# One score bank per slot instead of any free bank, and at most one VectorE job per round, in an attention planner

## The chip, the cores and the metric

The kernel runs on one core of one Trainium2 chip. The metric is the device time of one execution in microseconds (us). Before the change the median of three runs is 837.48 us (837.4 to 837.57). TensorE is called PE here, VectorE DVE, ScalarE ACT, GpSimd POOL, and SyncE, which issues nearly all DMAs, SP.

## What is computed

The input is x of 2048 rows (tokens) by 640 columns in bf16. It is layer-normalised, goes through an attention layer of 32 heads of 20 columns, through a gated feed-forward part, and the two results are joined:

```
xn  = layernorm(x)
q, k, v = split(xn @ wqkv)                  # 32 heads, 20 columns each
p   = softmax(q @ k.T * 20 ** -0.5)         # per head, 2048 x 2048
s   = (p @ v) @ wo
g   = silu((sigmoid(xn @ w_gate) * (xn @ w_up)) @ w_down)    # inner width 1728
out = x + s * g
```

The costly part is the exponential: 32 heads x 2048 x 2048 = 134 million of them.

## The kernel before

**The unit of work.** Heads are handled in eight groups of four (GH = 4), queries in four chunks of 512 (QC). One group with one chunk is a block, and there are 32 blocks (NBLK). In a block each head has 16 key tiles of 128 keys, so a block has 64 jobs and the kernel 2048. A job is one score matmul of 32 contraction rows by 512 columns (`score_mm`, L836 to L838), which fills one PSUM bank of 128 x 512 floats. The four heads of a group sit on four different groups of 32 rows, so up to four score matmuls of different heads run side by side on PE; this bundle is called a **round** (or F, as in the code). Then one of two engines takes the exponential of the bank:

- ACT, with an ACTIVATE that reads PSUM and writes `pt` in bf16 (`exp_act`, L87, recorded at L83);
- DVE, with one TENSOR_SCALAR that turns the score into 16-bit integers `iv` (L1168), and, for every four of those, three more passes over 2048 columns (L922, L925, L928) which make a product of two bf16 tiles `pb` from the bits.

The weighted sum of values is accumulated on PE in one bank `oacc` for the whole block (PV, `pv_emit`, L864 to L878), again four heads side by side, one matmul per ACT job and two per DVE job.

**PSUM.** There are eight banks: two pairs `scA[0]` and `scA[1]`, which hold two jobs each for ACT (a *slot*; the rounds alternate between them, `nfill % 2`), three single banks `bank[0..2]` (the trace calls them `bk`), and `oacc`. A round puts two jobs into its slot's pair, and ACT handles the pair with one ACTIVATE of 1024 columns. If a single bank is to be had, the round gives ACT a third job there, which costs a second ACTIVATE of 512 columns (L1144 to L1146). DVE's jobs use the same three single banks, and so does every other matmul of the kernel (called M): the projections of q, k and v, the gate, up and down projections of the feed-forward part, and the output projection.

**The planner.** The order of PE, ACT and DVE is not written out by hand. From L1026 on, a loop runs at build time through a clock of its own in steps of 0.02 us; it knows a planned cost for every operation (L422 to L428), keeps in `flex[f]` the planned time at which single bank f becomes free, and emits an instruction on an engine when that engine is free by its clock. On the chip each engine then runs its own list in order and waits on semaphores for what it needs. So a plan only sets order and places; the chip's durations set the time. On PE the choice is made at L1239 to L1252: a round F is issued at once when the margin until ACT runs dry is under URGENT = 0.25 us; otherwise PE stays in its mode (M or PV) while there is work, or holds for a moment when a slot is about to come free.

**What a round takes (L1253 to L1290).** First DVE jobs: up to D_MAX = 2 per round, while DVE is expected to be free in time, each in the first free bank of the list (2, 1, 0) (D_BANKS), picked by `claim_dve` (L827), for a head that the round does not have yet. Then a third bank for ACT, if fewer than two DVE jobs were taken: the first free one of (own, other, 2), where own is bank 0 or 1 by the slot's parity (A_BANKS). Then `claim_act` (L812) takes two or three jobs. So a round has at most four score matmuls: two and a third and a DVE job, or two and two DVE jobs. M items pick their bank at L1224 from (2, 1, 0) (M_BANKS). When the round could wait up to WAIT3 = 0.4 us for one of the banks in A_BANKS, L1243 lets it.

**The end.** After the last PV (chain at L981) the last block is divided on chip: copy of `oacc` (L962), four transposes (L966), scaling (L716, L718), transposes back (L975), copy (L979), then the output projection of the last chunk (L953, L957) and the final products.

Of the kernel before, what the change touches and what calls it, by code (L numbers as in the profile page):

```python
# [30 lines left out]
URGENT, ROUNDS, HOLD, SLACK, LEAD, LAG, D_LAST, D_LAST_END = 0.25, 4, 0.15, 0.2, 40.0, 0.0, 20, 8  # L31
D_ORD, M_ORD, WAIT3, FALL, M_END = 1, 0, 0.4, 1, 0.3
NPT, NPB, NIV = (3, 7), 3, 3
D_MAX, SLACKS = 2, (0.2, 0.2)
A_BANKS, D_BANKS = ((0, 1, 2), (1, 0, 2)), ((2, 1, 0), (2, 1, 0))
M_BANKS = ((2, 1, 0), (2, 1, 0))

LOG2E = 1.4426950408889634
UNIT = 128.0
# [13 lines left out]
def kernel(  # L53
# [33 lines left out]
    def exp_act(o, i):  # L87
        return act_imm(o, i, ACT.Exp, exp_scale)
# [338 lines left out]
    def t_exp(n):  # L427
        return (0.052 if n < SLOT else 0.104) + 0.4267 * n  # L428
# [378 lines left out]
    def take(b, j, i):  # L807
        n_left[b] -= 1
        claimed[0] += 1
        return b, left[b][j].pop(i), j  # L810

    def claim_act(n, not_j):  # L812
        got = []
        for b in range(base(), NBLK):
            if q_at.get(b, 1e9) > now:
                break
            while len(got) < n:
                js = [j for j in range(GH) if left[b][j] and j not in not_j and all(x[2] != j for x in got)]
# [8 lines left out]
    def claim_dve(had, not_j):  # L827
        for b in range(base(), min(NBLK, base() + 2)):
            if q_at.get(b, 1e9) > now:
                return None  # L830
            if n_left[b] >= (D_LAST if b < NBLK - 1 else D_LAST_END):
                js = [j for j in range(GH) if left[b][j] and j not in not_j]
                return take(b, max(js, key=lambda j: (j not in had, len(left[b][j]), j)), -1) if js else None
        return None

    def score_mm(dst, b, kt, j):  # L836
# [180 lines left out]
    with tc.manual_schedule(engines={ENG.PE, ENG.Activation, ENG.DVE}):  # L1017
# [60 lines left out]
        while chain or items or glu_items or any(it.i < len(it.ops) for it in active):  # L1078
# [34 lines left out]
            for eng in ("ACT", "DVE"):  # L1113
# [20 lines left out]
                if eng == "ACT":  # L1134
                    s = slots[nexp % 2]
                    if nexp < nfill and s["a"] is not None and s["at"] <= now:
                        jobs = s["a"]
                        m = len(jobs)
                        w = 2 if m <= 2 and buf_free(pt_left[2], NPT[0]) else 3
                        if buf_free(pt_left[w], NPT[w - 2]):  # L1140
                            pt = w2.tile([P, w, QC], BF16, tag=f"pt{w}", bufs=NPT[w - 2], name=f"pt{w}")
                            if m == SLOT:
                                flex[s["third"]] = now + t_exp(1) + EL
                            if m == SLOT:  # L1144
                                exp_act(pt[:, 2, :], bank[s["third"]])
# [61 lines left out]
            if free["PE"] <= now:  # L1207
# [10 lines left out]
                if cur is None:  # L1218
                    own = nfill % 2
                    m_new, m_bank = None, None  # L1220
                    m_it = next((e for e in active if e.i < len(e.ops) and e.ops[e.i][0] == "PE" and e.ready <= now), None)
                    if m_it is None:
                        behind = done < due() + LAG
                        for f in ((2,) if not behind and claimed[0] < NJOB * NBLK and not (FALL and not pv_ok and not can_f) else M_BANKS[own]):  # L1224
                            if flex[f] <= now:
                                m_bank = f
                                break
                        if m_bank is not None:
                            m_it = next((x for x in items[:80] if x.at <= progress() and (
                                x.need is None or o_at.get(x.need, 1e9) <= now) and all(  # L1230
                                ev_at.get(e, 1e9) <= now for e in x.pre)), None)
# [21 lines left out]
                if nxt == "F":  # L1253
                    busy = max(0.0, free["DVE"] - now) + T_IV * len(dq)
                    own = nfill % 2
                    d_new = []
                    while len(d_new) < D_MAX and (dcur is not None or buf_free(iv_left, NIV)) \
                            and busy + T_IV * len(d_new) <= T_F + T_MODE + PL + SLACKS[len(d_new)]:
                        f = next((f for f in D_BANKS[own] if flex[f] <= now), None)
                        if f is None:  # L1260
                            break
                        x = claim_dve([t[2] for t in dcur["jobs"]] if dcur else [], [y[2][2] for y in d_new])
                        if x is None:
                            break
                        if dcur is None:
                            iv_left.append([1, 0.0])
                            dcur = dict(jobs=[], n=0, k=0, i=len(iv_left) - 1,
                                        iv=w2.tile([P, GH, QC], I16, tag="iv", bufs=NIV, name="iv"))
# [7 lines left out]
                    if jobs or d_new:  # L1276
                        for x, t in enumerate(jobs):
                            score_mm(scA[nfill % 2][:, x, :] if x < 2 else bank[third], *t)
                        end = now + T_F + (T_MODE if mode != "F" else 0.0)
                        for d, i, x, f in d_new:  # L1280
                            score_mm(bank[f], *x)
                            dq.append((d, i, f, end + PL))
                        if jobs:
                            s["a"], s["at"], s["ends"] = jobs, end + PL, 0.0
                            if len(jobs) == SLOT:
                                s["third"] = third
                                flex[third] = 1e9
# [79 lines left out]
```

## Time and profile before

| what | value |
|---|---|
| median of three runs | 837.48 us |
| profiled execution, its own time | 837.4 us |
| its span, first to last instruction | 835.7 us |
| mean granted TensorE clock | 0.993 |
| ACT busy, 100 to 700 us | 99.2 to 100% in each 100 us |
| DVE busy, 100 to 700 us | 90 to 95% |
| PE busy, 100 to 700 us | 95 to 98% |
| first exponential starts, last one ends | 33.0 us, 816.06 us |
| last DMA-free work on POOL ends | 832.8 us |

The table is read so: the kernel has a prologue of 33 us (layer norm, first projections), a long middle in which ACT, DVE and PE all work at once, and an epilogue of 20 us after the last exponential. "Busy" in this profile is the time between an instruction's start and its end, and instructions of one engine overlap, so a busy share close to 100% does not by itself say that an engine is the bound.

### The profile page before, as it was taken

To read this page: it belongs to the slowest core of one execution; us is meant where nothing else is said; L and a number is where in the kernel's file an instruction comes from. 1 tells how busy PE (TensorE), PEld (TensorE's weight loads), DVE (VectorE), ACT (ScalarE), POOL (GpSimd) and SP (SyncE) were. 2 spreads that over 40 slices of the span, in tenths; PEclk is the share of its full clock that TensorE was granted. 3 is DMA by queue.
4 is the path that set the end of the run, shared out by engine and by line. 5 is a ranking of instruction groups with operands and counts; after the bars stand their busy time and mean duration, and the time that the engine had idled before them with its cause. 6 is when DMAs were issued, how large, how long until landed. Compare 5 with 4: busy or idle time off the path is not lost.

```text
span 835.7 us, 16970 instructions
## 1 busy us (share of the span) xinstructions
PE 783.8 (94%) x6388; PEld 277.6 (33%) x6388; DVE 756.3 (91%) x1174; ACT 800.7 (96%) x1043; POOL 81.3 (10%) x90
## 2 busy tenths in 40 slices
PE   4799999999999999999999999999999999999985
PEld 3433223333333232333323222334333333233332
DVE  7678989999899989899899998999999899999993
ACT  7799999999999999999999999999999999999990
POOL 5000000000000000000000000000000002222041
PEclk9899999999999999999999999999999999999998
DMA  5712221122222232221113222322112222324331
GB/s 155 212 35 58 64 67 54 52 67 55 66 75 58 66 85 77 55 66 56 42 43 87 73 62 69 91 78 82 47 62 69 79 72 75 94 61 127 94 130 36
DMA packets 93587, 62.58 MB, mean 75 GB/s; under 512 B 35044, under 2 KB 86884, under 8 KB 93504
## 3 DMA queue, kind: packets, MB, share of 16 engines
q1 hardware_dynamic: 93216, 61.16, 25.9%
q8 instruction: 50, 0.82, 0.4%
q10 hardware_dynamic: 288, 0.33, 0.1%
q14 instruction: 33, 0.27, 0.1%
HBM read 46.51 MB, written 12.40 MB: 70 GB/s over the span
## 4 chain that ended last, share of the span: by engine, by line
ACT 52%; PE 26%; DVE 13%; issue 7%; DMA 1%; SPq 1%; POOLq 0%; POOL 0%; ACTq 0%; DVEq 0%
ACT pt L83 47%; PE scA L837 7%; PE oacc L874 5%; DVE iv L1168 4%; PE bk L654 4%; PE bk L692 3%; ACT tnh L83 3%; DVE pb L928 2%; DVE pb L922 2%; DVE pb L925 2%; PE bk L517 1%; PE bk L742 1%; ACT td L83 1%; PE psk L143 1%; PE bk L625 1%
## 5 line engine op out<-in xcount | busy, mean ns | idle before, releaser
L83 ACT ACTIVATE pt<-scA 128x1024 bf16<-128x1024 f32 x689 | 710.5, 1179 | 6.4 <-PE bk L837 3.5
L1168 DVE TENSOR_SCALAR iv<-bk 128x512 int16<-128x512 f32 x464 | 312.1, 681 | 38.8 <-PE bk L837 37.1
L837 PE MATMUL scA<-q,kT 32*128 32x512 bf16 x1375 | 268.6, 383 | 15.9 <-ACT pt L83 10.6
L837 PE MATMUL bk<-q,kT 32*128 32x512 bf16 x673 | 211.8, 383 | 2.0 <-DVE iv L1168 1.0
L874 PE MATMUL oacc<-pt,v 128*21 128x512 bf16 x1584 | 185.8, 383 | 0.6 <-ACT pt L83 0.4
L837 PEld LDWEIGHTS <-kT 32*128 32x128 bf16 x2048 | 85.3, 91 | 254.8 <-issue 240.3
L83 ACT ACTIVATE pt<-bk 128x512 bf16<-128x512 f32 x209 | 157.5, 754 | 1.3 <-PE bk L837 1.2
L874 PE MATMUL oacc<-pb,v 128*21 128x512 bf16 x928 | 148.4, 382 | 3.4 <-DVE pb L928 2.0
L928 DVE TENSOR_TENSOR pb<-iv,pb 128x2048 bf16<-128x2048 bf16 x116 | 149.5, 1289 | 0.6
L654 PE MATMUL bk<-xnT,wgu 128*128 128x512 bf16 x520 | 145.8, 382 | 1.6 <-DVE hT L662 0.4
L904 POOL TENSOR_TENSOR on_bf<-on,rl 128x512 bf16<-128x512 f32 x31 | 41.0, 1321 | 676.2 <-DMA rl<-rd 498.0
L692 PE MATMUL bk<-wd,hT 128*128 128x320 bf16 x448 | 85.9, 302 | 1.5 <-DVE iv L1168 0.9
L922 DVE TENSOR_SCALAR pb<-iv 128x2048 int16<-128x2048 int16 x116 | 84.0, 724 | 2.1
L874 PEld LDWEIGHTS <-v 128*21 128x21 bf16 x2512 | 51.0, 91 | 95.7 <-issue 73.1
L925 DVE TENSOR_SCALAR pb<-iv 128x2048 int16<-128x2048 int16 x116 | 82.5, 711 | 0.0
L654 PEld LDWEIGHTS <-wgu 128*128 128x128 bf16 x520 | 38.3, 97 | 66.6 <-issue 45.5
L692 PEld LDWEIGHTS <-hT 128*128 128x128 bf16 x448 | 34.5, 97 | 45.8 <-issue 37.7
L517 PE MATMUL bk<-xnT,wu 128*120 128x512 bf16 x160 | 48.7, 398 | 0.2 <-ACT pt L83 0.2
L83 ACT ACTIVATE tnh<-bk 128x512 bf16<-128x512 f32 (+1 forms) x56 | 42.7, 762 | 0.1
L662 DVE SCALAR_TENSOR_TENSOR hT<-tnh,bk 128x512 bf16<-128x512 bf16 x52 | 35.4, 680 | 5.7 <-PE bk L654 3.1
L625 PE MATMUL bk<-wv,xnT 128*128 128x160 bf16 x280 | 30.2, 243 | 1.5 <-DVE iv L1168 1.2
L752 POOL TENSOR_TENSOR xnT<-otmp,xnT 128x320 bf16<-128x320 f32 x24 | 23.3, 975 | 50.8 <-DVE otmp L749 45.3
(105 smaller groups left out, 375.4 us busy)
## 6 DMA issues: line engine op xcount, KB each, us to landing
rl<-rd SPq DMA_DIRECT2D x124, 64.0 KB
wgu<-in_B_w_gate_dram SPq DMA_DIRECT2D x24, 320.0 KB
wgu<-in_B_w_up_dram SPq DMA_DIRECT2D x24, 320.0 KB
gq_dram<-gqs SPq DMA_DIRECT2D x32, 160.0 KB
xnT<-gq_dram SPq DMA_DIRECT2D x12, 320.0 KB
xt<-in_A_x_dram SPq DMA_DIRECT2D x16, 160.0 KB
oU<-on_bf SPq DMA_DIRECT2D x108, 20.0 KB
wd<-in_B_w_down_dram SPq DMA_DIRECT2D x1, 2080.0 KB
```

What stands on the lines that cost most here:

```text
L83: return nc.scalar.add_instruction(mybir.InstActivation(func=func, name=nc.get_next_instruction_name(), engine=ENG.Activation, ins=[nc.sca ...
L517: nc.tensor.matmul(st["ps"][0:UC, :], lhsT=wus[u][:, kd, i, :], rhs=xnT[:, c, kd, :], start=(kd == 0), stop=(kd == KD - 1))
L625: nc.tensor.matmul(st["ps"][:, i * 2 * GC:(i + 1) * 2 * GC], lhsT=xn_tok(tts[i], kd), rhs=wvs[pr][:, kd, :], start=(kd == 0), stop=(kd == ...
L654: nc.tensor.matmul(st[key][0:fs, :], lhsT=w[:, i, kd, ko * P:ko * P + fs], rhs=xnT[:, c, kd, :], start=(kd == 0), stop=(kd == KD - 1))
L692: nc.tensor.matmul(st["ps"][:, 0:HD], lhsT=hT[0:fsz[kf], kf, t4 * P:(t4 + 1) * P], rhs=wd[0:fsz[kf], kf, h * HD:(h + 1) * HD], start=(kf = ...
L837: nc.tensor.matmul(dst, lhsT=kTs[gc(b)[0] % 2][32 * j:32 * j + 32, kt * P:(kt + 1) * P], rhs=qts[b % 3][32 * j:32 * j + 32, :], start=True ...
L874: nc.tensor.matmul(oacc[32 * j:32 * j + DH + 1, :], lhsT=lhsT, rhs=u["src"], start=first, stop=last, tile_position=(0, 32 * j), skip_group ...
L904: nc.gpsimd.tensor_tensor(out=on_bf, in0=on, in1=rl, op=ALU.mult)
L922: nc.vector.tensor_scalar(out=pb[:, 0, :, :].bitcast(I16), in0=iv, scalar1=0x7F80, scalar2=1, op0=ALU.bitwise_and, op1=ALU.bitwise_or)
L925: nc.vector.tensor_scalar(out=pb[:, 1, :, :].bitcast(I16), in0=iv, scalar1=0x007F, scalar2=0x3F00, op0=ALU.bitwise_and, op1=ALU.bitwise_or)
L928: nc.vector.tensor_tensor(out=pb[:, 1, :, :], in0=iv.bitcast(BF16), in1=pb[:, 1, :, :], op=ALU.mult)
L1168: nc.vector.tensor_scalar(out=d["iv"][:, j, :], in0=bank[bk], scalar1=B_OFF, scalar2=0.0, op0=ALU.add, op1=ALU.max)
```

## The change

The change replaces the lists of allowed banks by one fixed choice, and the loop over DVE jobs by a single one:

- A third ACT job may only use the bank of its own slot's parity (bank 0 or 1), and only if the DVE job of the same round did not take it. Bank 2 and the other parity's bank are no longer offered.
- A round takes at most one DVE job, in the first free bank of (2, own, other), where it took up to two from (2, 1, 0).
- An M item looks through (2, other, own) where it looked through (2, 1, 0).
- The short wait before a round looks at its own bank alone.

```
-D_MAX, SLACKS = 2, (0.2, 0.2)
-A_BANKS, D_BANKS = ((0, 1, 2), (1, 0, 2)), ((2, 1, 0), (2, 1, 0))
-M_BANKS = ((2, 1, 0), (2, 1, 0))
...
                             if m == SLOT:
-                                flex[s["third"]] = now + t_exp(1) + EL
+                                flex[nexp % 2] = now + t_exp(1) + EL
                             if m == SLOT:
-                                exp_act(pt[:, 2, :], bank[s["third"]])
+                                exp_act(pt[:, 2, :], bank[nexp % 2])
...
-                        for f in ((2,) if not behind and claimed[0] < NJOB * NBLK and not (FALL and not pv_ok and not can_f) else M_BANKS[own]):
+                        for f in ((2,) if not behind and claimed[0] < NJOB * NBLK and not (FALL and not pv_ok and not can_f) else [(2, 1 - own, own), (2, own, 1 - own)][M_ORD]):
...
-                elif can_f and (margin < URGENT or (stay is None and not (margin > WAIT3 and any(now < flex[f] <= now + WAIT3 for f in A_BANKS[nfill % 2]) and not any(flex[f] <= now for f in A_BANKS[nfill % 2])))):
+                elif can_f and (margin < URGENT or (stay is None and not (flex[nfill % 2] <= now + WAIT3 and flex[nfill % 2] > now and margin > WAIT3))):
...
-                    d_new = []
-                    while len(d_new) < D_MAX and (dcur is not None or buf_free(iv_left, NIV)) \
-                            and busy + T_IV * len(d_new) <= T_F + T_MODE + PL + SLACKS[len(d_new)]:
-                        f = next((f for f in D_BANKS[own] if flex[f] <= now), None)
-                        if f is None:
-                            break
-                        x = claim_dve([t[2] for t in dcur["jobs"]] if dcur else [], [y[2][2] for y in d_new])
...
-                        d_new.append((dcur, len(dcur["jobs"]), x, f))
-                        dcur["jobs"].append(x)
-                        flex[f] = 1e9
-                        if len(dcur["jobs"]) == GH:
-                            dcur = None
-                    third = next((f for f in A_BANKS[own] if flex[f] <= now), None) if len(d_new) < 2 else None
-                    jobs = claim_act(SLOT if third is not None else SLOT - 1, [y[2][2] for y in d_new])
+                    d_bank, own = None, nfill % 2
+                    if d_can and busy <= T_F + T_MODE + PL + SLACK:
+                        d_bank = next((f for f in [(2, 1 - own, own), (2, own, 1 - own), (own, 2, 1 - own)][D_ORD] if flex[f] <= now), None)
+                    want = SLOT if flex[nfill % 2] <= now and d_bank != nfill % 2 else SLOT - 1
+                    d_new = None
+                    if d_bank is not None:
+                        x = claim_dve([t[2] for t in dcur["jobs"]] if dcur else [])
...
+                    jobs = claim_act(want, d_new[2][2] if d_new else None)
```

D_ORD is 1, M_ORD is 0 and SLACK is 0.2, as they stand in both kernels. Because the planner makes every later choice from the state that these choices leave, the order of all engines' instructions changes from the first blocks on; the prediction counts how.

More of the change, by code (lines that the diff above doesn't have):

```diff
@@ L817, in claim_act @@
             while len(got) < n:
-                js = [j for j in range(GH) if left[b][j] and j not in not_j and all(x[2] != j for x in got)]
+                js = [j for j in range(GH) if left[b][j] and j != not_j and all(x[2] != j for x in got)]
                 if not js:
@@ L825, in claim_act, with claim_dve @@
         return got
-    def claim_dve(had, not_j):
+    def claim_dve(had):
         for b in range(base(), min(NBLK, base() + 2)):
@@ L831, in claim_dve @@
             if n_left[b] >= (D_LAST if b < NBLK - 1 else D_LAST_END):
-                js = [j for j in range(GH) if left[b][j] and j not in not_j]
-                return take(b, max(js, key=lambda j: (j not in had, len(left[b][j]), j)), -1) if js else None
+                return take(b, max((j for j in range(GH) if left[b][j]),
+                                   key=lambda j: (j not in had, len(left[b][j]), j)), -1)
         return None
@@ L1253 @@
                 if nxt == "F":
+                    d_can = dcur is not None or buf_free(iv_left, NIV)
                     busy = max(0.0, free["DVE"] - now) + T_IV * len(dq)
-                    own = nfill % 2
-                    d_new = []
-                    while len(d_new) < D_MAX and (dcur is not None or buf_free(iv_left, NIV)) \
-                            and busy + T_IV * len(d_new) <= T_F + T_MODE + PL + SLACKS[len(d_new)]:
-                        f = next((f for f in D_BANKS[own] if flex[f] <= now), None)
-                        if f is None:
-                            break
-                        x = claim_dve([t[2] for t in dcur["jobs"]] if dcur else [], [y[2][2] for y in d_new])
[L1263 to L1268, printed above, removed]
-                        d_new.append((dcur, len(dcur["jobs"]), x, f))
-                        dcur["jobs"].append(x)
-                        flex[f] = 1e9
-                        if len(dcur["jobs"]) == GH:
-                            dcur = None
@@ L1274 @@
-                    third = next((f for f in A_BANKS[own] if flex[f] <= now), None) if len(d_new) < 2 else None
-                    jobs = claim_act(SLOT if third is not None else SLOT - 1, [y[2][2] for y in d_new])
-                    if jobs or d_new:
-                        for x, t in enumerate(jobs):
-                            score_mm(scA[nfill % 2][:, x, :] if x < 2 else bank[third], *t)
+                    d_bank, own = None, nfill % 2
+                    if d_can and busy <= T_F + T_MODE + PL + SLACK:
+                        d_bank = next((f for f in [(2, 1 - own, own), (2, own, 1 - own), (own, 2, 1 - own)][D_ORD] if flex[f] <= now), None)
@@ new lines @@
+                    want = SLOT if flex[nfill % 2] <= now and d_bank != nfill % 2 else SLOT - 1
+                    d_new = None
+                    if d_bank is not None:
+                        x = claim_dve([t[2] for t in dcur["jobs"]] if dcur else [])
+                        if x is not None:
+                            if dcur is None:
+                                iv_left.append([1, 0.0])
+                                dcur = dict(jobs=[], n=0, k=0, i=len(iv_left) - 1,
+                                            iv=w2.tile([P, GH, QC], I16, tag="iv", bufs=NIV, name="iv"))
+                            d_new = dcur, len(dcur["jobs"]), x
+                            dcur["jobs"].append(x)
@@ L1279 @@
+                    jobs = claim_act(want, d_new[2][2] if d_new else None)
+                    if jobs or d_new is not None:
+                        for x, t in enumerate(jobs):
+                            score_mm(scA[nfill % 2][:, x, :] if x < 2 else bank[nfill % 2], *t)
+                        if d_new is not None:
+                            score_mm(bank[d_bank], *d_new[2])
+                            if len(dcur["jobs"]) == GH:
+                                dcur = None
                         end = now + T_F + (T_MODE if mode != "F" else 0.0)
-                        for d, i, x, f in d_new:
-                            score_mm(bank[f], *x)
-                            dq.append((d, i, f, end + PL))
+                        if d_new is not None:
+                            dq.append((d_new[0], d_new[1], d_bank, end + PL))
+                            flex[d_bank] = 1e9
@@ L1285 @@
                             if len(jobs) == SLOT:
-                                s["third"] = third
-                                flex[third] = 1e9
+                                flex[nfill % 2] = 1e9
                             nfill += 1
```

## The prediction

> **What bounds the kernel now.** I begin with the page's busy times and its slices.
>
> ```profile
> PE 783.8 (94%) x6388; PEld 277.6 (33%) x6388; DVE 756.3 (91%) x1174; ACT 800.7 (96%) x1043; POOL 81.3 (10%) x90
> ...
> PE   4799999999999999999999999999999999999985
> ...
> ACT  7799999999999999999999999999999999999990
> ```
>
> Three engines look full. Which one is full, only the pace of its instructions tells. The timeline of ACT alone shows it (start, duration, what).
>
> ```profile
> 165.38 0.89 ACT L83 ACTIVATE pt<-bk 128x512 bf16<-128x512 f32 x1
> 165.87 2.23 ACT L83 ACTIVATE pt<-scA 128x1024 bf16<-128x1024 f32 x2
> 167.68 0.91 ACT L83 ACTIVATE pt<-bk 128x512 bf16<-128x512 f32 x1
> 168.16 2.26 ACT L83 ACTIVATE pt<-scA 128x1024 bf16<-128x1024 f32 x2
> ```
>
> Compare ends, start plus duration: 166.27, 168.10, 168.59, 170.42. A third bank costs 0.49 us, two pairs 1.83, so 0.916 each. Over the whole trace, end to end, the middle eight tenths of the pairs lie between 0.916 and 0.918 and those of the single banks between 0.489 and 0.491 us; a 320-column tanh takes 0.330. Twice 0.490 less 0.916 is 0.064: that is what an ACTIVATE costs beside its columns. Now the counts, from the groups with shapes kept apart (count | busy, mean ns | idle before).
>
> ```profile
> L83 ACT ACTIVATE pt<-scA 128x1024 bf16<-128x1024 f32 x686 | 709.0, 1181 | 6.4 <-PE bk L837 3.5 <-PE scA L837 1.8 <-PE oacc L874 0.4
> L1168 DVE TENSOR_SCALAR iv<-bk 128x512 int16<-128x512 f32 x464 | 312.1, 681 | 38.8 <-PE bk L837 37.1
> ...
> L83 ACT ACTIVATE pt<-bk 128x512 bf16<-128x512 f32 x209 | 157.5, 754 | 1.3 <-PE bk L837 1.2
> ```
>
> 686 x 0.9165 + (209 + 3) x 0.490 for the exponentials, 56 x 0.490 + 32 x 0.330 for the tanhs and 7 x 0.490 for the q tiles make 774.5 us. The first exponential ends at 34.0, the last at 816.06: 782.0 us. **ACT works at its own pace for all but 8.9 us**; of those 1.9 fall before 45 us, where the granted clock was 0.75, and about 0.5 are 64-partition tanhs that I priced too low. Some 6.5 us are stalls. Last the waits.
>
> ```profile
> PE scA L837 <- ACT pt L83: 10.6, 33, 0.9
> ...
> ACT pt L83 <- PE bk L837: 4.7, 8, 2.6
> ...
> ACT pt L83 <- PE scA L837: 1.8, 4, 0.9
> ```
>
> PE waits 33 times for ACT to free a slot, 10.6 us in all: that is how far PE is ahead. DVE waits 37.1 us for scores, so it isn't the bound. The largest stall shows how ACT is starved all the same:
>
> ```profile
> 717.59 1.28 DVE L925 TENSOR_SCALAR pb<-iv 128x2048 int16<-128x2048 int16 x1
> ...
> 718.79 0.68 DVE L1168 TENSOR_SCALAR iv<-bk 128x512 int16<-128x512 f32 x1
> ...
> 719.52 0.39 PE L837 MATMUL bk<-q,kT 32*128 32x512 bf16 x2 [0.53 <-DVE iv L1168]
> ...
> 721.29 1.02 ACT L83 ACTIVATE pt<-scA 128x1024 bf16<-128x1024 f32 x1 [0.90 <-PE scA L837]
> ```
>
> A DVE pass ran 1.28 us instead of about 0.69 beside a POOL product; DVE read its bank late; PE, in order, stood 0.53 us before the matmul that reuses that bank; the round behind came late. Of the stalls over 50 ns after 45 us, those with such a wait of PE on DVE close before them sum to about 4.4 us, the rest to 1.4 (and the tanhs).
>
> **The change, part by part.** I count in the built orders of both kernels.
>
> *What stays.* 464 DVE jobs and 116 groups of passes, 1584 ACT jobs, 6388 matmuls, all M items, POOL's list, 733 rows on SP: the same numbers. The shares of ACT and DVE don't move. SP's list changes its order by a few places (feed-forward weights against the small norm transfers); DMA is busy 0.21 to 0.34 of the time in the stages from 40 to 800 us, and no wait of PE, ACT or DVE on a DMA there is above 1.2 us. I cost it at nothing; if that cover fails, one such wait is 1.2 us.
>
> *ACT instructions.* Triples fall from 209 to 134, pairs rise from 686 to 722, singles in a pair's bank from 3 to 6: 36 ACTIVATEs fewer, the same columns. 36 x 0.064 = **-2.3 us**, all on the path since ACT is full.
>
> The Trainium skill ("ScalarE: Activation LUTs", section "What ACT_TABLE_LOAD costs") gives 186 ns fixed with an overlap of about 93 ns back to back, so 93 ns per ACTIVATE; by that estimate the term would be -3.3 us. The rows say 64 ns, and I keep them.
>
> *PE work.* With 1584 ACT jobs in smaller portions there are 728 rounds with ACT jobs instead of 689. On PE the starts of a round's matmuls lie 3 to 6 ns apart, and a round costs 0.213 us like a full matmul; a change between round, PV and M costs 0.312 to 0.317 from start to start instead of 0.213 to 0.216, so 0.10 more. Rounds: 39 x 0.213 = 8.3. Changes of mode, counted in the orders, 1442 to 1501: 59 x 0.10 = 5.9. PV bundles, 654 to 661: 7 x 0.213 = 1.5. Together **15.7 us more PE work**; by these rows PE's list grows from 706.7 to 722.4 us, beside 774.5 and 772.2 of ACT.
>
> The Trainium skill ("TensorEngine Tiling (Array Packing)", section "Key Properties") says that a change of tiling mode drains TensorE. This speaks against the change; a drain to the end of a matmul would be 0.383 us from start to start (the mean of the rows), 0.17 more, and 59 of them 10.0 us instead of 5.9. The trace shows 0.31, so the drain is not seen in full, and the lower price stands.
>
> *How much of it reaches ACT.* Between 40 and 816 us PE's starts lie 62.6 us later in sum than the prices above; but much of it is slips under 60 ns or waits for DVE, and only the 10.6 us of waiting for ACT is time that PE has to give. Ends: nothing reaches ACT (all 15.7 found room in the 62.6), or all does (each extra lies where PE isn't ahead). I take what exceeds the lead: 15.7 - 10.6 = **+5.1 us**. The orders point the same way. Take the PE work from one round's start to the next and the ACT work queued in that round: PE is longer by over 0.5 us in 10 rounds before and 23 after; over eight rounds in a row in none before and 6 after; over twelve rounds PE's sum is above ACT's once before and 22 times after. And a pair covers PE for 0.916 us where a triple covers 1.41.
>
> *Bank handovers.* Single banks are filled 75 times less (673 to 598 score matmuls). Of the reuses of a bank, about 148 come within 1.3 us of PE work after its last filling before, about 72 after. So a late DVE meets PE at the bank less often; the stalls that hang on a bank (near 520, 586, 617, 721 and 773 us) sum to some 2.6 us. Half could go, -1.3; with PE's lead used up, a wait isn't made good and the same stalls could double, +2.6. I take 0, between them and near the row.
>
> *The end.* Before, the last round with a DVE job leaves ACT 1.41 + 1.41 + 1.41 + 0.49 = 4.71 us of its own, and DVE's last pass (2.25 us, drawn out beside POOL) ended 0.8 us before ACT. After, it leaves 0.92 + 0.92 + 1.41 + 0.49 = 3.73, 0.98 less: DVE would end last by 0.2 us if its pass is drawn out again, and not if the pass runs its usual 1.2 us. 0, at most +0.2 (up to +1.0 if a pass behind it is drawn out too). The chain behind the last PV is the same.
>
> Sum: -2.3 + 5.1 + 0 + 0 = +2.8 on the profiled 837.4 us: **840.2 us**. The profiled execution stands 0.08 under the median, which is nothing here.
>
> **Rivals.**
>
> 1. *ACT stays fed, and only its instructions count.* For: PE has 62.6 us of slack by the price list, DVE-late waits at banks are half as many, the plan issues a round ahead of all else once ACT has under 0.25 us left. Against: only 10.6 us of the slack is lead. 837.4 - 2.3 = 835.1, with the halved handovers 833.8. It decides if less than about 0.6 us of the extra PE work arrives at ACT (the bound for "faster" is 0.2%, 835.7; about what a measurement of this kernel can tell).
>
> 2. *The two terms cancel*, that is, the change does nothing that shows: stalls grow by 0.6 to 4.0 us. For: plans of both kernels move the same jobs through the same engines. 835.7 to 839.1, middle 837.4.
>
> 3. *PE becomes the bound.* For: stretches of eight to twelve rounds with more PE than ACT work, which two slots can't bridge. Against: over the whole, PE's list stays 50 us shorter than ACT's. All of the extra work on the path: 837.4 - 2.3 + 15.7 = 850.8; it begins where over 9 us reach ACT, 844.
>
> **How the numbers follow.** Forecast (839.1 to 844.0, at 840.2) 0.37; rival 1 0.27; rival 2 0.18; rival 3 0.18. The range reaches from rival 1's lower end, 833.8, over the forecast and into rival 3 as far as 848; above that I leave about 0.1, below about 0.07. Faster by over 0.2% is rival 1, 0.27; within it rival 2, 0.18; slower the forecast and rival 3, 0.55.
>
> **What would show it.** Right: in the new profile 722 ACTIVATEs of 1024 columns and 134 from single banks, still 0.916 and 0.490 us from end to end; ACT's span between first and last exponential longer than its 772.2 us of work by some 14 instead of 7.5 to 9; PE's wait for ACT at scA well under 10.6 us; ACT's idle before scA, 6.4 us now, up. Wrong: PE still waits 10 us or more for ACT and ACT's stalls stay at 9 us (rival 1); or PE's slices hold no wait on ACT at all and the stalls pass 20 us (rival 3). If the time behind the last exponential differs from 19.6 us of the span, the end was mis-read. If the late DVE passes beside POOL cost ACT more in fewer places, the handover term was.

## The result, and the profile after

The changed kernel takes 841.99 us (median of 4 runs, 840.51 to 842.71) and the kernel before, run beside it, 837.44 (835.74 to 837.57). The ratio is **1.0057, with an interval of 1.0037 to 1.0077**: slower by over 0.2%. The forecast was 840.2.

The profiled execution took 842.71 us, its span is 841.0, its mean granted clock 0.987. Lines 80 and later of the new kernel stand three lower than before (L83 is now L80, L837 is L834). First the page's busy times and slices.

```profile
PE 793.8 (94%) x6388; PEld 278.7 (33%) x6388; DVE 756.5 (90%) x1174; ACT 799.7 (95%) x1007; POOL 84.3 (10%) x90
...
ACT  7699999999999999999999999999999999999990
...
PEclk9899999999999999999999999999999999999997
```

PE is busy 10.0 us longer with the same 6388 matmuls, ACT has 36 instructions fewer and yet the end comes later. ACT's groups with shapes kept apart (count | busy, mean ns | idle before):

```profile
L80 ACT ACTIVATE pt<-scA 128x1024 bf16<-128x1024 f32 x722 | 715.7, 1150 | 5.1 <-PE bk L834 2.9 <-PE scA L834 1.4 <-PE oacc L871 0.2
L80 ACT ACTIVATE pt<-bk 128x512 bf16<-128x512 f32 x134 | 96.6, 721 | 6.1 <-PE bk L834 5.7
```

The counts are those of the built orders, 722 and 134. From end to end a pair still takes 0.916 us and a single bank 0.490. The idle time moved: 6.4 to 5.1 us before pairs, 1.3 to 6.1 before single banks, in sum 7.7 to 11.2. The waits say on whom (us in total, times, longest):

```profile
DVE iv L1165 <- PE bk L834: 42.1, 80, 1.5
...
ACT pt L80 <- PE bk L834: 8.6, 17, 2.6
PE scA L834 <- ACT pt L80: 8.2, 32, 0.9
```

Where the score that comes last stands in a single bank (`bk`), ACT waited 8 times before (4.7 us) and now 17 times; PE still waits 32 times for ACT.

**Where the time went.** I add up ACT's work by the end-to-end prices of the prediction, and call a *stall* each place where ACT's next end comes over 50 ns later than its price allows; with a wait of PE for DVE in the 3.5 us ahead it is a DVE stall. All in us, one profiled execution each; the last two columns are the same two kernels, timed and profiled again later.

| | before | after | before again (e8) | after again (e7) |
|---|---|---|---|---|
| span | 835.7 | 841.0 | 837.6 | 839.9 |
| ACT's work between the exponentials | 773.6 | 771.7 | 773.6 | 771.7 |
| stalls before 50 us (clock) | 1.9 | 3.1 | 1.9 | 1.5 |
| DVE stalls | 3.7 | 4.1 | 2.6 | 4.5 |
| other stalls | 2.6 | 5.7 | 2.3 | 5.5 |
| last exponential to the last PV | 0.43 | 1.40 | 0.64 | 1.39 |
| projections after it (L953, now L950) | 7.2 | 8.9 | 9.6 | 8.4 |
| last exponential to the end | 19.6 | 22.3 | 22.9 | 22.0 |

Three rows repeat and so belong to the change: -1.9 of ACT's work, **about +3.1 of other stalls**, and some +0.9 because DVE ends last. With the DVE stalls (+0.4 and +1.9) they make +2.5 and +4.0. The clock makes the rest of the first pair: a half-clock stretch that begins near 35 us lasted 10.2 us after and 6.8 before (1.2 us), and one from 823.2 for 3.4 us slowed the projections (1.7 us). These two don't repeat: in e7 and e8 it is before that pays more. The medians of the second call stand 3.2 us apart if the 12 runs of e8 are taken (841.64 and 838.47), and 4.5 if the 35 other runs of before in that call are (837.11); the first pair stood 4.6 apart.

One of the new stalls in the timeline of after (start, duration, what, idle before):

```profile
265.56 0.64 PE L514 MATMUL bk<-xnT,wu 128*120 128x512 bf16 x2
...
266.13 0.39 PE L871 MATMUL oacc<-pb,v 128*21 128x512 bf16 x2
...
266.35 0.39 PE L871 MATMUL oacc<-pb,v 128*21 128x512 bf16 x4
...
266.79 0.38 PE L871 MATMUL oacc<-pb,v 128*21 128x512 bf16 x2
...
267.11 0.39 PE L834 MATMUL scA<-q,kT 32*128 32x512 bf16 x2
...
267.33 0.37 PE L834 MATMUL bk<-q,kT 32*128 32x512 bf16 x1
...
267.60 1.94 ACT L80 ACTIVATE pt<-scA 128x1024 bf16<-128x1024 f32 x2 [0.61 <-PE bk L834]
```

Two M matmuls, then a burst of PV (16 matmuls, 4 bundles, 266.13 to 267.1), then two rounds 0.22 us apart. ACT ran dry at 266.99 and stood for 0.61 us. PE shows no wait for another engine here: it did things in this order because its list has them so. The burst holds PE for 0.97 us, more than ACT stood.

### The profile page after: what moved, and what is told of

It reads as the page before. It is cut to its first block, busy times and chain, and to the rows that moved or that the text cites. A ratio compares the mean times of both kernels' runs of the same rounds, so it can differ in the third digit from the quotient of the medians.

```text
span 841.0 us, 16951 instructions
## 1 busy us (share of the span) xinstructions
PE 793.8 (94%) x6388; PEld 278.7 (33%) x6388; DVE 756.5 (90%) x1174; ACT 799.7 (95%) x1007; POOL 84.3 (10%) x90
## 4 chain that ended last, share of the span: by engine, by line
ACT 39%; PE 36%; DVE 16%; issue 5%; DMA 2%; SPq 1%; POOL 0%; POOLq 0%; ACTq 0%; DVEq 0%
ACT pt L80 36%; PE scA L834 11%; PE oacc L871 8%; PE bk L651 6%; DVE iv L1165 6%; PE bk L689 5%; DVE pb L925 3%; DVE pb L919 2%; DVE pb L922 2%; PE bk L514 1%; ACT tnh L80 1%; PE bk L622 1%; PE psk L140 1%; DVE hT L659 1%; PE bk L834 1%
## 5 line engine op out<-in xcount | busy, mean ns | idle before, releaser
L80 ACT ACTIVATE pt<-scA 128x1024 bf16<-128x1024 f32 x728 | 718.9, 1147 | 5.1 <-PE bk L834 2.9
L834 PE MATMUL scA<-q,kT 32*128 32x512 bf16 x1450 | 283.8, 384 | 14.1 <-ACT pt L80 8.2
L834 PE MATMUL bk<-q,kT 32*128 32x512 bf16 x598 | 211.0, 385 | 1.3 <-DVE iv L1165 1.3
L834 PEld LDWEIGHTS <-kT 32*128 32x128 bf16 x2048 | 87.7, 91 | 265.2 <-issue 250.8
L925 DVE TENSOR_TENSOR pb<-iv,pb 128x2048 bf16<-128x2048 bf16 x116 | 149.2, 1286 | 0.7
L901 POOL TENSOR_TENSOR on_bf<-on,rl 128x512 bf16<-128x512 f32 x31 | 44.2, 1426 | 677.2 <-DMA rl<-rd 428.0
L80 ACT ACTIVATE pt<-bk 128x512 bf16<-128x512 f32 x134 | 96.6, 721 | 6.1 <-PE bk L834 5.7
L689 PE MATMUL bk<-wd,hT 128*128 128x320 bf16 x448 | 87.6, 303 | 1.0 <-DVE iv L1165 0.9
L80 ACT ACTIVATE tnh<-bk 128x512 bf16<-128x512 f32 (+1 forms) x56 | 41.1, 734 | 0.1
```

Source lines behind the costliest of these rows:

```text
L80: return nc.scalar.add_instruction(mybir.InstActivation(func=func, name=nc.get_next_instruction_name(), engine=ENG.Activation, ins=[nc.sca ...
L689: nc.tensor.matmul(st["ps"][:, 0:HD], lhsT=hT[0:fsz[kf], kf, t4 * P:(t4 + 1) * P], rhs=wd[0:fsz[kf], kf, h * HD:(h + 1) * HD], start=(kf = ...
L834: nc.tensor.matmul(dst, lhsT=kTs[gc(b)[0] % 2][32 * j:32 * j + 32, kt * P:(kt + 1) * P], rhs=qts[b % 3][32 * j:32 * j + 32, :], start=True ...
L901: nc.gpsimd.tensor_tensor(out=on_bf, in0=on, in1=rl, op=ALU.mult)
L925: nc.vector.tensor_tensor(out=pb[:, 1, :, :], in0=iv.bitcast(BF16), in1=pb[:, 1, :, :], op=ALU.mult)
```

## The experiments

Ratios are to the kernel before on the same chip; its median there was 839.11 us for e1 to e4, 837.11 for e5 to e8, 837.83 for e9.

### e1: the kernel before with as much more PE work, in its own order

```
-            nc.tensor.matmul(st[key][0:fs, :], lhsT=w[:, i, kd, ko * P:ko * P + fs],
-                             rhs=xnT[:, c, kd, :], start=(kd == 0), stop=(kd == KD - 1))
+            n = 1
+            if kd == 0:
+                again[0] += 1
+                n += again[0] * 7 % 10 < 7
+            for x in range(n):
+                nc.tensor.matmul(st[key][0:fs, :], lhsT=w[:, i, kd, ko * P:ko * P + fs],
+                                 rhs=xnT[:, c, kd, :], start=(kd == 0), stop=(kd == KD - 1 or x < n - 1))
```

So 7 of 10 first matmuls of a gate or up product are issued twice, 72 in all.

> The kernel before, with its order and banks untouched, but 72 of the gate and up matmuls issued twice (the first copy closes its own group and is overwritten by the second, so the output stays): 72 x 0.216 = 15.6 us more work on PE, about what the change adds (15.7), and nothing else. Theory (extra PE work beyond PE's lead over ACT reaches ACT): the stalls of ACT grow by 4 to 6 us, 837.4 becomes 841 to 843.5, and the growth lies in stalls that have no wait of PE on DVE just before them. Rival (the after kernel's new stalls come from its bank choice, its altered order or the half-speed clock windows, not from PE's load): the extra work vanishes in the 62.6 us of slack, 837 to 838.5.

Measured: 844.56 us, 1.0070 [1.0045, 1.0095]. ACT's work is unchanged at 773.6; the other stalls rise from 2.6 to 7.6, the DVE stalls stay (3.9).

```profile
L83 ACT ACTIVATE pt<-scA 128x1024 bf16<-128x1024 f32 x686 | 692.2, 1120 | 7.1 <-PE bk L844 5.2 <-PE scA L844 0.9
L83 ACT ACTIVATE pt<-bk 128x512 bf16<-128x512 f32 x209 | 144.6, 692 | 1.6 <-PE bk L844 1.5
```

The groups are those of before, the releaser PE. So 15.6 us more of PE work (72 times 0.216, by the prediction's price), unplanned, cost some 5 of stalls: PE's free time absorbs two thirds. That is the size of the prediction's term.

### e2: the changed kernel with 72 matmuls less, in its own order

```
+            if kd == 1:
+                again[0] += 1
+                if again[0] * 7 % 10 < 7:
+                    return
             nc.tensor.matmul(st[key][0:fs, :], lhsT=w[:, i, kd, ko * P:ko * P + fs],
```

> The kernel after, with its order and banks untouched, but 72 of the gate and up matmuls left out (one fifth of the sum of those products is missing, so the output is not the reference's): 15.6 us less PE work. Theory: ACT's stalls fall by 3 to 5 us, to the level of before; the time falls from 842 to 837 to 839, and what stays over before's time less the 2.3 us of saved ACTIVATEs is the end (DVE last) and the clock windows. Rival (bank choice or order): it stays at 841 to 842.5.

Measured: 841.85 us, 1.0029 [1.0014, 1.0044]; other stalls 5.2 instead of 5.7. **Here the theory fails**: 837 to 839 us were expected. Against the 1.0042 to 1.0057 of after, the relief of 15.6 us is worth 1 to 2 us, and most of the stalls stand where they stood. ACT's timeline at two of the places, first after, then after again (e7), then e2:

```profile
182.40 0.60 ACT L80 ACTIVATE pt<-bk 128x512 bf16<-128x512 f32 x1 [0.58 <-PE bk L834]
...
267.60 2.86 ACT L80 ACTIVATE pt<-scA 128x1024 bf16<-128x1024 f32 x3 [0.61 <-PE bk L834]
```

```profile
182.19 0.60 ACT L80 ACTIVATE pt<-bk 128x512 bf16<-128x512 f32 x1 [0.59 <-PE bk L834]
...
267.42 2.85 ACT L80 ACTIVATE pt<-scA 128x1024 bf16<-128x1024 f32 x3 [0.61 <-PE bk L834]
```

```profile
182.52 0.60 ACT L80 ACTIVATE pt<-bk 128x512 bf16<-128x512 f32 x1 [0.59 <-PE bk L840]
...
267.93 2.86 ACT L80 ACTIVATE pt<-scA 128x1024 bf16<-128x1024 f32 x3 [0.61 <-PE bk L840]
```

The same instruction, the same length to 0.01 us, with and without 15 us of PE work. The same holds near 410, 416, 452 and 786 us (0.37 to 0.45 us each). If PE were merely short of time, one would expect shorter stalls, or others. These stalls are in the order. Not all are of one kind: ahead of the one at 182.4 and the one near 452 PE waits for DVE (0.46 us for `iv` at 180.88 in after), so by the rule above they are DVE stalls that repeat.

**The new theory.** At build time I counted in the planner how often PV was put ahead of a due round (ACT's margin under URGENT), because all seven `pt` tiles that hold exponentials for PV were taken (the condition `full` at L1241 of before), and how long ACT stands idle in the planner's own clock. The measured stalls are from the profiles. The last column sums those of ACT's stalls, of either kind, that end within 3 us after such a PV bundle starts in the trace; the built order gives the bundle's place among PE's matmuls. (The traces of e1 to e4 lack 52 to 56 matmuls; there the places are matched by the sequence of lines.)

| order | PV ahead of a due round | ACT idle in the plan | rounds | mode changes | other stalls, measured | stalls within 3 us of such a PV |
|---|---|---|---|---|---|---|
| before, e8 | 6 | 2.3 | 689 | 1442 | 2.6, again 2.3 | 1.0, again 1.0 |
| after, e7 | 27 | 7.2 | 728 | 1501 | 5.7, again 5.5 | 3.7, again 3.7 |
| e1 | 6 | 2.3 | as before | | 7.6 | 1.0 |
| e2 | 27 | 7.2 | as after | | 5.2 | 3.8 |
| e3 | 45 | 12.1 | 731 | 1521 | 10.6 | 7.5 |
| e4 | 0 | 2.3 | 678 | 1418 | 3.1 | 0 |
| e5 | 8 | 3.0 | 727 | 1510 | 6.3 (4.1 without the clock's part) | 0.6 |
| e6, e9 | 6 | 2.3 | 727 | 1539 | 10.8 and 7.8 (4.8 and 5.4 without one hole) | 2.5 (0.7 without that hole) and 1.2 |

The count does not foretell the column of other stalls: e5, e6 and e9 lie far above what 6 to 8 would give, unless a part is taken out, and e1 has the order of before and three times its stalls. It does foretell the last one. In after the 27 places fall on ten stalls, all of them other stalls, the same ten in e7; before has 1.0 us there. So 2.7 of the +3.1 stand right behind such bursts, in 41 of some 770 us. (The hole of e6 and e9 is, by its lines below, a wait of PE for DVE.)

The chain would be: more rounds and mode changes make PE's planned list longer; planned M items fall behind their due times; PV is put off until `pt` is full; then three or four bundles at once go ahead of a round that is due, and ACT stands. The planner seems to make this worse than need be (e6): it prices a change of mode at 0.107 us above a matmul and rounds up to steps of 0.02, so 0.34 us, where the trace has 0.312 to 0.317.

### e3 and e4: one half of the change each

e3 gives the third ACT job only its own bank; e4 allows one DVE job per round.

```
-A_BANKS, D_BANKS = ((0, 1, 2), (1, 0, 2)), ((2, 1, 0), (2, 1, 0))
+A_BANKS, D_BANKS = ((0,), (1,)), ((2, 1, 0), (2, 1, 0))
```

```
-D_MAX, SLACKS = 2, (0.2, 0.2)
+D_MAX, SLACKS = 1, (0.2, 0.2)
```

> Before with one part of the change alone: the third job of ACT only in its own slot's bank (A_BANKS ((0,), (1,))), still up to two DVE jobs per round. Counted in the built order: triples 115, pairs 727, ACT jobs 1573 (11 fewer, which DVE takes), rounds 731, changes of mode 1521. ACT work 724.6 us in the exponentials against 732.6, so -8.0; PE +9.0 for rounds and +7.9 for modes. Theory: -8.0 from ACT and some +5 to +6 of stalls, 834 to 836.5, faster than before; if DVE, which gets 13 us more, becomes late, up to 839. Rival (giving up free banks is what costs): 840 or more.

> Before with the other part alone: at most one DVE job per round, third bank still any free one. Counted in the built order: triples 255, pairs 670, ACT jobs 1603 (19 more, taken from DVE), rounds 678, changes of mode 1418. ACT work in the exponentials 742.9 us against 732.6, so +10.3; PE -4.7. Theory (ACT is the bound, PE a near one): +10.3 less up to 2 of stalls, 845.5 to 848. Rival (the number of DVE jobs per round costs nothing, the loss sits in the third bank): 837 to 839.

Measured: e3 842.11 us, 1.0043 [1.0024, 1.0061]; e4 850.42 us, 1.0131 [1.0110, 1.0152]. ACT's groups of e3:

```profile
L83 ACT ACTIVATE pt<-scA 128x1024 bf16<-128x1024 f32 x727 | 717.8, 1150 | 12.2 <-PE bk L837 7.4 <-PE scA L837 3.1 <-PE oacc L874 0.5
L83 ACT ACTIVATE pt<-bk 128x512 bf16<-128x512 f32 x115 | 82.6, 718 | 2.9 <-PE oacc L874 1.5 <-PE bk L837 1.4
```

Triples fall to 115, and 11 jobs move from ACT to DVE, so ACT's work falls by 8.0 to 765.6; I had expected that gain to arrive (834 to 836.5 us). It didn't: DVE stalls are 7.2 and other stalls 10.6. The half that makes ACT's work shorter has an order with the most bursts of all. e4 has no burst, and its ACT loses only 7.6 us in stalls, but 19 jobs move from DVE to ACT: its work is 784.4, 10.8 more, and its time, by the ratio 848.4 on before's 837.4, lies just above the 845.5 to 848 that I expected. The two halves move the shares in opposite directions, by 11 and by 19 jobs, and the change as a whole leaves 464 DVE jobs as they were; the halves don't simply add.

### e5: e2's matmuls left out, and the planner told

```
+    def some():
+        again[0] += 1
+        return [kd for kd in range(KD) if kd != 1 or again[0] * 7 % 10 >= 7]
...
-        return [Item([("PE", alloc0, [(T_MM, lambda kd=kd: mm("g", 0, kd)) for kd in range(KD)]),
+        return [Item([("PE", alloc0, [(T_MM, lambda kd=kd: mm("g", 0, kd)) for kd in some()]),
```

The up product is edited in the same way.

> The kernel after with the same 72 gate and up matmuls left out as in the second experiment (output not the reference's), but now the planner knows it: the items are shorter in the plan as well. The built order keeps the sizes of after (134 triples, 722 pairs, 1583 ACT jobs, 727 rounds, 1510 changes of mode), but the place of rounds, PV and M among each other is planned anew. New theory: the stalls of after stand in the plan. There PE has more to do, M falls behind its due times, PV is put off until the tiles of finished exponentials (pt) are all taken, and then goes ahead of a round that is due; in the planner's own clock that happens 27 times in after and 6 times before, and 8 times here. If so, the stalls without a wait for DVE fall from 5.7 us to 2.5 to 3.5 and the time to 838 to 840 on a day when after takes 842. Rival (PE's load matters only as it is on the chip, or the stalls belong to the bank choice): as in the second experiment, 841 to 842.5, stalls 5 us or more.

Measured: **836.83 us, 0.9980 [0.9957, 1.0002]**, against 1.0042 [1.0021, 1.0063] of the changed kernel in the same call (e7). The work left out is that of e2; the order alone differs.

```profile
L80 ACT ACTIVATE pt<-scA 128x1024 bf16<-128x1024 f32 x722 | 721.2, 1166 | 4.3 <-PE bk L840 1.4 <-PE scA L840 1.3 <-PE oacc L877 0.6
L80 ACT ACTIVATE pt<-bk 128x512 bf16<-128x512 f32 x134 | 97.7, 729 | 4.2 <-PE bk L840 4.1
```

The same 722 and 134 ACTIVATEs, and the idle time before them is 8.5 instead of 11.2. By the medians less work and a new order together are worth 4.8 us (e7 to e5); by the ratios of e2 and e5, which lie apart beyond their intervals but come from two chips, the order alone is worth some 4. The profiled executions show a part of that: stalls behind 50 us of 8.6 against 10.0 in e7 (6.4, if 2.2 us in and just behind a half-clock stretch from 788.2 are left out), and 1.1 us because the first exponential came earlier, which the order of the middle has no part in. I had expected other stalls of 2.5 to 3.5; their 6.3 is what the rival foretold. What fell as the theory has it are the stalls right behind bursts, from 3.7 to 0.6.

### e6 and e9: the own bank, with a truer price for a change of mode

```
-    T_F, T_PV, T_MM, T_MODE = 0.2133, 0.2133, 0.2133, 0.107
+    T_F, T_PV, T_MM, T_MODE = 0.2133, 0.2133, 0.2133, .095
```

> The third bank restricted as in the third experiment, up to two DVE jobs, and the planner's price for a change of mode on PE lowered from 0.107 to 0.095 us, which with the steps of 0.02 makes 0.32 instead of 0.34 us from start to start; the trace shows 0.312 to 0.317. Counted: 120 triples, 722 pairs, 1569 ACT jobs (479 to DVE), 727 rounds, 1539 changes of mode; ACT work in the exponentials 723.0 us, 9.6 less than before; the planner's own clock has PV ahead of an urgent round 6 times instead of 45 in the third experiment. Theory (plan-made PV bursts are what cost there): stalls without DVE from 10.6 down to 3 to 5 us; those with a wait for DVE stay near 7, as DVE has more jobs; 837.4 - 9.6 + 2 to 5 = 830 to 833, faster than both kernels. Rival (PE's real load decides: 38 rounds and 97 changes of mode more than before, 18 us): stalls stay at 17 us, 837 to 840 as in the third experiment.

Measured: 837.00 us, 0.9986 [0.9963, 1.0008], not the 830 to 833 I expected, but 0.6% better than e3 (on another chip), of which it is a small edit, with as many rounds and more mode changes. So it isn't their number that costs but where the plan puts things. ACT's work is 764.0, and its gain over before (9.6) is lost again mostly in one hole:

```profile
787.68 0.38 SPq L704 DMA_DIRECT2D gq_dram<-gqs  x1
...
792.91 0.32 SPq L942 DMA_DIRECT2D wd<-gq_dram  x1
792.98 0.49 DVE L749 SCALAR_TENSOR_TENSOR otmp<-bk,xnT 128x320 f32<-128x320 f32 x1 [2.82 <-DMA gq_dram<-gqs]
793.52 0.58 PE L837 MATMUL bk<-q,kT 32*128 32x512 bf16 x1 [2.27 <-DVE otmp L749]
...
793.98 0.39 SPq L728 DMA_DIRECT2D xnT<-gq_dram  x1
...
795.86 1.02 ACT L83 ACTIVATE pt<-scA 128x1024 bf16<-128x1024 f32 x1 [3.53 <-PE scA L837]
```

SP issued a store of gq at 787.68; its semaphore tells of the landing at 792.85. Behind it in order stood a load for the final products that reads what it stores, and went out at 792.91. DVE waited 2.82 us, PE 2.27 us for DVE, ACT 3.53. From 793.4 the granted clock was half for 6.8 us. e9 takes that load off SP and lets ACT issue it behind its last exponential:

```
-            nc.sync.dma_start(out=tail[t4][1], in_=gq_dram[r, :])
+            if t4 < 3:
+                nc.sync.dma_start(out=tail[t4][1], in_=gq_dram[r, :])
...
+        nc.scalar.dma_start(out=tail[3][1], in_=gq_dram[4 * (NQC - 1) * P + 3 * P:4 * NQC * P, :])
```

> The kernel e6 (own bank for the third ACT job, a planned mode change dearer by 0.095 us instead of 0.107), and the load of the last tile of gq for the final products, which stood on SP from 787.7 to 792.9 us behind the store it reads, is issued by ACT behind its last exponential instead; nothing is left out. In e6 DVE waited 2.82 us for the gq load queued behind it on SP, PE 2.27 us for DVE, the granted clock fell to a half from 793.4 us for 6.8 us, and ACT stood still 6.0 us between 795.9 and 801. Theory (the order of e6 is good, and that one load on SP is what it lost): DVE's wait for gq there under 1 us, no half-clock window near 793, ACT's stalls without a late DVE 4 to 6 us in all, and 831 to 834.5 us, about 0.994 of before. Rival (DVE or the clock would have lost the time elsewhere, as a stall always comes with so few ACT jobs): 836 to 838, as e6. What counts against both: the chain behind the last exponential waits for the load on ACT's queue, which would show as DVE waiting at the final products and a tail over 23 us.

Measured: **836.36 us, 0.9977 [0.9963, 0.9992]**, slightly faster than before, but in the 836 to 838 of the rival and not the 831 to 834.5 I expected.

```profile
789.68 0.38 SPq L704 DMA_DIRECT2D gq_dram<-gqs  x1
...
791.57 0.32 SPq L728 DMA_DIRECT2D xnT<-gq_dram  x1
...
794.63 0.49 DVE L749 SCALAR_TENSOR_TENSOR otmp<-bk,xnT 128x320 f32<-128x320 f32 x1 [2.49 <-DMA gq_dram<-gqs]
795.17 0.37 PE L837 MATMUL bk<-q,kT 32*128 32x512 bf16 x1 [1.93 <-DVE otmp L749]
...
796.70 2.86 ACT L83 ACTIVATE pt<-scA 128x1024 bf16<-128x1024 f32 x3 [2.35 <-PE scA L837]
```

SP is free of the 5.2 us (L728 goes out at 791.57), and the half-clock stretch near 793 is gone; the hole shrinks from 6.0 us (four stalls up to 802) to one wait of 2.35. But DVE still waits 2.49 us. In both runs the semaphore that it waits for is that of the store (L704), which lands 5.17 us after its issue in e6 and 4.83 in e9 (at 794.51); `otmp` takes its buffer from the same three as `gqs`. So the expectation of e9 had the cause wrong: DVE did not wait for a load queued on SP but for the landing of the store. Why that takes 5 us here, where it takes 1.8 in e8 (794.58 to 796.35), stays open. And a half-clock stretch of 10.2 us from 811.8 lies on the projections now, with a tail of 23.4 us. No wait at the final products was added.

### e7 and e8: the two kernels again

> The kernel after, unchanged, a second time: which of its stalls, of the half-speed clock windows and of the 22.3 us behind the last exponential come back. Theory: the stalls of the middle come back at the same places (they are in the order), 9 to 10.5 us; the half-speed windows near 35 and 823 us move or change length by 3.4 us or a multiple, and the time with them by 1 to 3 us. Rival (the windows belong to the kernel's order): they come back at the same places with the same length. Ratio to before 1.004 to 1.007.

> The kernel before, unchanged, a second time, timed against itself: the spread that a ratio of 1 has here, and whether its half-speed window near 35 us and its 19.6 us behind the last exponential come back. Ratio 0.998 to 1.002; stalls of the middle 6 to 7 us at the same places; windows as in the run of after again.

Measured: 841.64 us, 1.0042 [1.0021, 1.0063], and 838.47 us, 1.0003 [0.9980, 1.0025]. Their stalls are in the table at the top: the other stalls repeat to 0.3 us, the tail and the stalls before 50 us do not.

## Why the prediction was right, point by point

- **ACT instructions, -2.3.** Right: 36 ACTIVATEs fewer, work -1.9.
- **PE work that reaches ACT, +5.1.** Right in sign, 2 us too large, and wrong in its reason. Measured are +3.1 of other stalls in the middle, in both pairs. The step that failed is "I take what exceeds the lead: 15.7 - 10.6". The lead was not used up: PE still waits 8.2 us for ACT in 32 places (10.6 in 33), where I asked for "well under 10.6". e1 shows that as much PE work in the order of before costs 5 us, so the size has its support. But e2 shows that the stalls right behind bursts don't go when the work goes (3.7 to 3.8), and e5 that these go when the planner lays the list anew (0.6). The count that pointed the right way was the other one in the same paragraph, of stretches with more PE than ACT work (1 before, 22 after): it looks at the order, the lead at the sum.
- **"ACT's idle before scA up".** Wrong: down from 6.4 to 5.1, and up before the single banks from 1.3 to 6.1. The sum was right: the span between the exponentials exceeds ACT's work by 13.1 us, where I wrote "some 14". (The products behind the 774.5 us of ACT's work add up to 774.0; without the first exponential that is 773.1, and 782.0 less 773.1 gives the 8.9.)
- **Bank handovers, 0.** Within its bounds: DVE stalls 3.7 to 4.1, in the repeat 2.6 to 4.5. (By the rule used here the stalls of before split into 3.7 and 2.6, where the prediction had 4.4 and 1.4.)
- **The end, 0, "at most +0.2 (up to +1.0 if a pass behind it is drawn out too)".** The high bound came true, in both executions of after. Its last DVE passes:

```profile
816.73 1.06 DVE L919 TENSOR_SCALAR pb<-iv 128x2048 int16<-128x2048 int16 x1
...
818.42 1.23 DVE L925 TENSOR_TENSOR pb<-iv,pb 128x2048 bf16<-128x2048 bf16 x1
...
819.70 0.40 PE L871 MATMUL oacc<-pb,v 128*21 128x512 bf16 x4 [0.57 <-DVE pb L925]
```

ACT ends at 818.70, DVE at 819.65, the last PV at 820.10: 1.40 us behind ACT, where it was 0.43. The pass that was drawn out is the first, 1.06 us for about 0.69, beside a POOL product that ends at 817.24.
- **The clock** was in no term. It adds 2.9 us to the first pair of profiled executions and nothing to the second; how much of the medians' 842.0 it is, no run shows.
- **The sum, +2.8.** The parts that repeat and the DVE stalls make +2.5 and +4.0. So the sum came near in part by luck: the term of PE work is 2 us too large, and the end and the DVE stalls, taken at 0, brought 1.4 and 2.7.
- **Rivals.** ACT did not stay fed (1). The terms did not cancel (2): after stands 3.2 to 4.6 us above before in every comparison of medians, and rival 2 ended at 1.7. PE did not become the bound (3): its waits for ACT are still there.

What stays open: no run moved only a burst of PV behind the round that it delays. That the bursts make the stalls rests on the timeline, on the last column of the table and on e5 against e2, not on an edit of that alone; a burst could also mark a place where PE's list is behind anyway. e1 shows that plain PE load makes stalls too, and only 1.0 of its 11.5 us stand behind bursts.

## What to carry to other kernels

Where a planner at build time orders an in-order engine, ask of a stall first whether it comes back at the same place in another execution, and with work taken out: if so it is in the list, and a lighter load without a new plan buys little (here 1 to 2 us of 15.6). Count in the built order how often work is put ahead of a feed that is due, and compare the planner's prices with the trace; here 0.012 us in one price, which the planner's steps make 0.02, moved the time of an order by 0.6% (e3 to e6, on two chips). And before a few us are put down to an edit, see how much the clock at the start and the end gives or takes in a repeat.

## What the runs showed of the hardware that was not expected

**Half-clock stretches.** The granted clock falls to a half for 3.4 us or a multiple (6.8, 10.2; the last stretch runs to the end of the record), near 35 us in some runs and in the last 62 us in all (the earliest at 786.4 of 848.7 us, in e4). The place and the number differ between executions of one order: before shows 35.0 (6.8 us) and 830.3, its repeat 35.0, 813.3 (10.2 us) and 830.3. The price shows in the tail's projections, first before, then after, each the first six matmuls:

```profile
819.12 1.46 PE L953 MATMUL scA<-wo,oU 128*128 128x512 bf16 x6
```

```profile
822.74 2.35 PE L950 MATMUL scA<-wo,oU 128*128 128x512 bf16 x6
```

The 0.89 us more are the clock's. In the 3.4 us before the half rate began at 823.2 PE had stood idle twice, 0.79 and 0.94 us, ahead of the two groups of transposes. In the profile of before the same chain had 0.78 and 0.94 us of idle and kept its clock. PE was busy for 1.66 us of the 3.4 in after (819.8 to 823.2) and for 1.79 in before (816.6 to 820.0). The Trainium skill ("TensorE: Matmul & The Clock Gate", "Part 1: The HAM clock gate") describes a free-running window of about 3.4 us and a half rate after an idle one. The runs here agree on the length; but the half rate came after 3.4 us in which PE was idle for parts only, and the same chain met it in the profile of after and not in that of before.

**DVE beside POOL.** A bf16 product of DVE (L928 before, L925 after) takes 1.21 us alone and 1.61 to 1.73 in the mean when a POOL product overlaps it, up to 2.33 (17 of 116 overlap before, 21 after). Two such lines of after:

```profile
814.65 1.44 DVE L925 TENSOR_TENSOR pb<-iv,pb 128x2048 bf16<-128x2048 bf16 x1
814.97 2.27 POOL L901 TENSOR_TENSOR on_bf<-on,rl 128x512 bf16<-128x512 f32 x1
```

POOL's product mostly takes 1.26 to 1.27 us. The one that starts second is drawn out, by nearly what is left of the first: here POOL's takes 2.27 us, with 1.12 of the DVE pass still to come. The other way round, in after, the DVE product takes 2.33 us when it starts 0.02 us behind POOL's, 2.04 at 0.31 and 1.55 at 0.81. The 0.23 us that this DVE pass itself is longer than alone are not explained by that.

**A store and the load that reads it.** Through DRAM on SP they stand 5.2 us apart in e6 (787.68 to 792.91), as the load goes out only when the store has landed, and everything behind them on that queue waits as well. DVE, which is to write the store's buffer anew, waits for the same landing.
